# Chunk 0 of a fused attention and MoE kernel in two parts, with chunk 1 between them

## The chip, the cores and the metric

The kernel runs on one core of one Trainium2 chip. The metric is the device time of one execution, in microseconds (us); the profile of one execution gives a span from its first to its last instruction, which is a little shorter than the device time. Engines are named as the profile names them: PE (TensorE, matmuls), DVE (VectorE), ACT (ScalarE), POOL (GpSimd) and SP (SyncE, which here issues the DMAs).

## The reference

Four batches of eight heads, 576 positions, head width 64. Each head's output is a local attention (a band of seven positions) plus a coarse attention over means of four positions, repeated fourfold. The result, 2304 tokens of 512, goes through a two-layer MLP with a Mish-like gate; its weights are float64.

```python
def _attn_ref(q, k, v):
    ...
    q_d = q.reshape(B, H, Sd, factor, D).mean(axis=3)
    ...
    out_up = np.repeat(sm_attn(q_d, k_d, v_d), factor, axis=2)
    mask = np.abs(pos[:, None] - pos[None, :]) < factor
    scores = np.where(mask, scale * np.matmul(q, k.transpose(0, 1, 3, 2)), -1000000000.0)
    ...
    return (out_up + np.matmul(attn, v)).astype(np.float32)

def _moe_ref(x, w_in, w_out):
    h = x @ w_in
    sp = np.where(h > 20.0, h, np.log1p(np.exp(np.minimum(h, 20.0))))
    return ((h * np.tanh(sp)) @ w_out).astype(np.float32)
```

## The kernel before, in words

Attention is done in units of one batch and one pair of heads (four pairs a batch, 16 units). A unit loads `qk` and `vv` by DMA (L417, L503), reduces and scores on PE (`sc`, `sl`), does both softmaxes on DVE and ACT, lets POOL sum `vv` (L506, L508, into `vd`), transposes (`at`, `pt`, `pve`) and multiplies on PE (`pvo`, and L566, 72 small matmuls into `pve` and `pvo`). DVE adds both parts (L579), ACT rounds the sum to the high part of x (L597) and DVE subtracts for the low part (L599). From the fifth unit on all units share one set of buffers, so a unit's `vv` can be loaded only when the unit before has done its L566.

The MLP runs over six chunks of 384 tokens and 16 tiles `f` of 128 hidden columns. Batch 0 (576 tokens) is chunk 0 and the first half of chunk 1; batch 1 is the other half of chunk 1 and chunk 2. Chunks 0 and 1 go in *slots*, one slot a chunk and an `f`: 12 matmuls `h<-x,wi` (four pairs times three combinations of high and low parts, L785), Mish and its high part on ACT (L809, L814), the low part on DVE (L815), and nine matmuls `acc<-wo,g` (L828) into three PSUM banks, which hold a chunk's sums from its first `f` to its last. After the last `f` ACT and DVE copy the banks to `stg` tiles and SP stores them (L838 to L844). Chunks 2 to 5 go in *quartets*, a Strassen scheme of seven products (L746), with the sums of x made from chunks in DRAM (`far`, `sa`, `fars`, `q`).

A weight tile comes as 64-bit words. For each `wi` and `wo` of an `f`: one DMA of 512 KB (L628), ACT scales the high words (L630), DVE shifts the low ones (L632), joins both (L634, into an `stg` tile `full`), ACT or DVE makes the rounded high part (L640 or L638), DVE the low part (L641). Seven `stg` tiles are shared with the outputs and the sums.

The order of the instructions on every engine is written out by a planner inside the kernel: each operation has an assumed duration, a due time (`prio`, in slots) and its dependences, and the planner picks on each engine the due operation that can run. The constants at the head of the file (ATT, UNIT, WPRI, LAG and so on) shift the due times. Where PE would idle in the plan, it puts fillers: matmuls on the identity (`warm`, 512 columns, before the first slot; 128 columns into the unused end of an `h` bank after it). The order is fixed when the program is built; on the chip the engines wait for each other by semaphores. Each engine, and SP's list of DMAs, takes its own in order.

Of the kernel before, what the change touches and what calls it, by code (L numbers as in the profile page):

```python
# [9 lines left out]
F32 = mybir.dt.float32  # L10
# [5 lines left out]
ALU = mybir.AluOpType  # L16
# [3 lines left out]
P = 128  # L20
BIG = 1e30
CH = 384
LAG = (0.1, 6.06, 26.18)
FA = 5
SETS = 3
ATT = {0: (-842.3, 62.6), 1: (2.8, 3.8), 2: (-7.2, 5.7), 3: (-35.9, 5.6)}
WPRI = (-2.33, 7.84, 15.62)
UNIT = {(0, 0): -55, (1, 3): -15, (0, 3): 10, (1, 2): -8, (0, 2): 23, (1, 1): -38, (0, 1): 67, (1, 0): 5, (3, 3): 8, (2, 3): -11, (3, 2): 0, (2, 0): 2, (2, 2): 12, (3, 0): 2, (2, 1): 5, (3, 1): -22}
WARM = True
NPRO = 4  # L30
WACT = 184
STICK = 34
VOFF = 1
WDMA = -65
PIPE0 = (1, 0, 1)
PIPE1 = (1, 0, 1)
LEAD = 3
PMASK = (0, 1)
AMUL = ((0, 2), (1, 0), (1, 1))
AEXP = ((0, 2),)  # L40
WHI = ((0, 'wo'), (2, 'wo'), (7, 'wi'), (8, 'wi'), (11, 'wi'), (12, 'wi'), (14, 'wo'), (15, 'wi'), (15, 'wo'))
RDV = ((0, 0), (0, 1), (0, 2), (0, 3), (1, 0), (1, 3), (2, 0), (3, 0), (3, 2), (3, 3))
GHI = (9, 10, 12, 13, 14, 16, 17, 18, 20, 23, 24, 25, 30)
NMISH = (4,)
TAIL = 0
SPRE = 44
SPRE2 = 104
JPRE = -45
XDMA = -45
QPRE = -15  # L50
QPRE2 = 100
QSTEP = 0.6
QDMA = 51
SUMS = 2
TPRE = 92
UPRE = -20
KEEP = 121
LOAD, PRE = 1320, 250
TICK, BUSY, PACE = 3413.3, 3900, 4900
KW = 38  # L60
RATE, LAND = 415.0, 1100
# [35 lines left out]
class Plan:  # L97
# [9 lines left out]
    def op(self, eng, dur, fn, r=(), w=(), prio=None, after=(), cold=None, cols=0, gap=0, two=True, ins=6, tab=None):  # L107
        o = Op()
        o.eng, o.dur, o.fn, o.cold, o.cols, o.gap, o.two, o.ins, o.tab = eng, dur, fn, cold or 2 * dur, cols, gap, two, ins, tab
        o.prio = self.prio if prio is None else prio  # L110
        o.deps, o.bufs, o.outs, o.seq, o.raw, o.hold = set(after), [], [], len(self.ops), set(), 0.0
        for items, writes in ((r, False), (w, True)):
            for x in items:
                b, key = x if isinstance(x, tuple) else (x, None)
                write = writes or b.group.endswith("ps")
                if b not in o.bufs:
                    o.bufs.append(b)
                    b.left += 1
                for k, (wr, rd) in b.marks.items():
                    if key is None or k is None or k == key:  # L120
                        o.deps.update(wr)
                        o.raw.update(wr)
                        if write:
                            o.deps.update(rd)
                if write:
                    if key is None:
                        b.marks = {None: ({o}, set())}
                    else:
                        b.marks[key] = ({o}, set())
                else:  # L130
                    b.marks.setdefault(key, (set(), set()))[1].add(o)
        o.deps.discard(o)
        self.ops.append(o)
        return o
# [192 lines left out]
def dve(n, fast=False):  # L327
    return 69 + (0.52 if fast else 1.042) * n
# [10 lines left out]
class Kernel:  # L339
# [59 lines left out]
    def attention(self, b, p, sb, ps, padded, loose):  # L399
# [62 lines left out]

        pmask = b in PMASK or (b, p) in AEXP

# [149 lines left out]
    def load_w(self, f):  # L614
# [6 lines left out]
        for nm, src in (("wi", wi), ("wo", wo)):  # L621
            pl.prio = prio + (WPRI[2] if nm == "wo" else 0)
            raw = pl.buf("wa" if f < FA else "wb", f"{nm}{f}", [P, 512, 2], I32, 1, f"raw_{nm}{f}")
# [6 lines left out]
            op("act", act(512), lambda hi=hi: nc.scalar.activation(  # L630
                hi().bitcast(F32), hi().bitcast(F32), AF.Prelu, scale=2.0 ** -112, alpha=2.0 ** 32), w=[h], prio=pl.prio + WACT, tab="exp")
            op("dve", dve(512, True), lambda lo=lo: nc.vector.tensor_scalar(  # L632
# [158 lines left out]
    def tail(self, s, c, f, h, own=None, place=("mish", "g"), last=None):  # L791
        nc, pl = self.nc, self.plan
        op = pl.op
        last = f == self.NF - 1 if last is None else last
        if own is None:
            G, psum = pl.buf("mish", "mA", [P, CH], F32, NMISH[0], f"mA{s}"), True
            Gv, Hv = G, h
            H, h = [[(b, m) for m in range(3)] for b in (G, h)]
        else:
            H, Gv, Hv, psum = h, own, own, False  # L800
        g = pl.buf(*place, [P, 2, CH], F32R, 3 if place[0] == "x" else 2, f"g{s}")
        parts = [(0, CH, None)] if s < 95 - TAIL else [(i * P, (i + 1) * P, i) for i in range(3)]

        for c0, c1, key in parts:
            n, o_ = c1 - c0, slice(c0, c1)
            pl.prio = s + 0.2
            x_, h_ = [b if key is None else [b[key]] for b in (H, h)]
            one, two = [(g, 2 * (key or 0) + j) for j in range(2)]
            op("act", act(n, psum), lambda o_=o_: nc.scalar.activation(Gv()[:, o_], Hv()[:, o_], AF.Mish),  # L809
               r=h_, w=x_, tab="mish")  # L810
            if s in GHI:
                op("dve", dve(n, True), lambda o_=o_: nc.vector.tensor_copy(g()[:, 0, o_], Gv()[:, o_]), r=x_, w=[one])
            else:
                op("act", act(n), lambda o_=o_: nc.scalar.activation(g()[:, 0, o_], Gv()[:, o_], AF.Copy), r=x_, w=[one])  # L814
            op("dve", dve(n), lambda o_=o_: nc.vector.tensor_tensor(  # L815
                out=g()[:, 1, o_], in0=Gv()[:, o_], in1=g()[:, 0, o_].bitcast(F32), op=ALU.subtract), r=[*x_, one], w=[two])
        wo = self.w["wo", f]
        first = c not in self.acc
        if first:
            where, tag = ("attps", "att1") if c in (3, 5) else ("moeps", None)  # L820
            self.acc[c] = [pl.buf(where, tag or f"acc{i}", [P, 512], F32, self.nb[where, tag] if tag else 1, f"acc{s}_{i}")
                           for i in range(3)]
        for i in range(3):
            a_ = self.acc[c][i]

            def mm2(i=i, a_=a_, first=first, last=last):
                for j, (a, b_) in enumerate(((0, 0), (0, 1), (1, 0))):
                    nc.tensor.matmul(a_(), g()[:, a, i * P:(i + 1) * P], wo()[:, b_],  # L828
                                     start=first and j == 0, stop=last and j == 2)

            gi = [g] if len(parts) == 1 else [(g, 2 * i), (g, 2 * i + 1)]
            op("pe", 700, mm2, r=[*gi, wo], w=[a_], cols=1536, prio=s + LAG[(s >= 20) + (s >= 60)] - 0.5 + 0.1 * i)
            if not last:
                continue
            o = pl.buf("stg", "stg", [P, 512], F32, self.nstg, f"o{c}_{i}")
            ov, ok = o, o
            if i % 2:
                op("dve", dve(512), lambda a_=a_, ov=ov: nc.vector.tensor_copy(ov(), a_()),  # L838
                   r=[a_], w=[ok], prio=s + 1, two=False)
            else:  # L840
                op("act", act(512, True), lambda a_=a_, ov=ov: nc.scalar.activation(ov(), a_(), AF.Copy),
                   r=[a_], w=[ok], prio=s + 1)
            r0 = c * CH + i * P
            op("sp", P * 2048 / RATE, lambda r0=r0, ov=ov: nc.sync.dma_start(self.out[r0:r0 + P, :], ov()), r=[ok], prio=s + 1)  # L844

    def run(self, ctx):
        tc = self.tc
        nc, pools = self.nc, {}
# [27 lines left out]
        for b in (0, 1):  # L876
            for p in range(self.NPAIR):
                if len(units) == NPRO:
                    break
                units.append((ATT[b][0] + ATT[b][1] * p + UNIT.get((b, p), 0), self.attention(  # L880
                    b, p, sets[len(units) % len(sets)], ("props", "attps"),
# [2 lines left out]
        gate = list(pl.ops)  # L884
        n0 = len(pl.ops)
        for f in range(self.NF):
            pl.prio = WPRI[0] + WPRI[1] * f
            self.load_w(f)

        todo = [(c, f) for c in range(2) for f in range(self.NF)]  # L890
        s = 0

        def slots(todo):
            nonlocal s
            for c, f in todo:
                self.slot(s, c, f)
                s += 1

        def units(bs):
            us = [(ATT[b][0] + ATT[b][1] * p + UNIT.get((b, p), 0), self.attention(b, p, "att", "attps", probs["att"], False))  # L900
                  for b in bs for p in range(self.NPAIR) if 4 * b + p >= NPRO]
            self.record(us, PIPE1)

        units((1,))
        slots(todo[:16])
        units((2, 3))
        self.sums(2)
        slots(todo[16:32])
        self.operands(2)
        for i in range(self.NF // 2):  # L910
            self.quartet(32 + 4 * i, i, 2)
# [84 lines left out]
```

## Time and profile before

| what | us |
|---|---|
| median of three runs | 497.84 (495.67 to 500.41) |
| the profiled execution's own time | 497.26 |
| its span, first to last instruction | 495.5 |

The profile lists for each engine the time in which it was busy and what ended its idle time. Matmuls overlap, so a row of n matmuls starts the next row a little before its own end; PEld are weight loads, which run beside the matmuls. "PEclk" is the granted clock as a share of 2.4 GHz. Names are `out<-in`, with the buffer numbers left out.

### The profile page before, as it was taken

To read this page: it belongs to the slowest core of one execution; us is meant where nothing else is said; L and a number is where in the kernel's file an instruction comes from. 1 tells how busy PE (TensorE), PEld (TensorE's weight loads), DVE (VectorE), ACT (ScalarE), POOL (GpSimd) and SP (SyncE) were. 2 spreads that over 40 slices of the span, in tenths; PEclk is the share of its full clock that TensorE was granted. 3 is DMA by queue.
4 is the path that set the end of the run, shared out by engine and by line. 5 is a ranking of instruction groups with operands and counts; after the bars stand their busy time and mean duration, and the time that the engine had idled before them with its cause. 6 is when DMAs were issued, how large, how long until landed. Compare 5 with 4: busy or idle time off the path is not lost.

```text
span 495.5 us, 11601 instructions
## 1 busy us (share of the span) xinstructions
PE 479.5 (97%) x4728; PEld 412.8 (83%) x4728; DVE 361.2 (73%) x821; ACT 281.2 (57%) x642; POOL 43.5 (9%) x70
## 2 busy tenths in 40 slices
PE   7889999999999999999999999999999999999996
PEld 3667877878788888888898999889989999888885
DVE  4999998999975586667896867656949877653511
ACT  2598999858575597766544334334735444343411
POOL 7501001112021111011000000000000000000000
PEclk9999999999999999999999999999999999999999
DMA  8976996355444687525311410101430000000003
GB/s 344 419 291 243 411 413 244 123 176 179 141 142 155 216 276 243 194 69 182 105 32 33 141 36 16 33 16 39 123 127 1 0 2 1 1 0 1 0 1 127
DMA packets 23381, 65.60 MB, mean 132 GB/s; under 512 B 2592, under 2 KB 12832, under 8 KB 21280
## 3 DMA queue, kind: packets, MB, share of 16 engines
q1 hardware_dynamic: 23328, 64.86, 36.3%
q8 instruction: 37, 0.61, 0.5%
q14 instruction: 16, 0.13, 0.1%
HBM read 53.84 MB, written 11.01 MB: 131 GB/s over the span
## 4 chain that ended last, share of the span: by engine, by line
PE 81%; ACT 9%; DVE 7%; issue 2%; POOL 1%; ACTq 0%; DVEq 0%; POOLq 0%
PE acc L828 37%; PE h L746 24%; PE h L785 9%; PE sc L433 2%; PE pve L566 2%; PE sl L472 2%; PE pt L551 1%; ACT raw_wi L630 1%; ACT L809 1%; PE pvo L538 1%; ACT raw_wo L630 1%; PE at L517 1%; DVE qkd L418 1%; ACT mA L809 1%; ACT A L440 1%
## 5 line engine op out<-in xcount | busy, mean ns | idle before, releaser
L828 PE MATMUL acc<-wo,g 128*128 128x512 f32 x864 | 219.3, 395 | 0.0
L828 PEld LDWEIGHTS acc<-wo,g 128*128 128x128 f32 x864 | 159.3, 188 | 28.4 <-issue 0.4
L753 DVE TENSOR_TENSOR u<-h,u 128x384 f32<-128x384 f32 x112 | 61.0, 552 | 30.6 <-ACT g L814 14.8
L785 PE MATMUL h<-x,wi 128*128 128x384 f32 x384 | 75.6, 344 | 2.4 <-ACT mA L809 1.4
L785 PEld LDWEIGHTS h<-x,wi 128*128 128x128 f32 x384 | 66.0, 188 | 5.6 <-ACT mA L809 2.1
L814 ACT ACTIVATE g<-u 128x384 fp32r<-128x384 f32 (+1 forms) x66 | 33.6, 513 | 57.5 <-PE acc L828 57.1
L809 ACT ACTIVATE u<-u 128x384 f32<-128x384 f32 (+1 forms) x66 | 33.8, 515 | 52.0 <-DVE u L753 51.8
L815 DVE TENSOR_TENSOR g<-u,g 128x384 fp32r<-128x384 f32 (+1 forms) x66 | 35.4, 541 | 35.0 <-ACT g L814 35.0
L746 PE MATMUL h<-x,t 128*128 128x384 f32 x192 | 39.9, 338 | 0.6 <-DVE u L753 0.6
L506 POOL TENSOR_TENSOR vv<-vv 128x512 f32<-128x512 f32 x16 | 22.8, 1423 | 184.0 <-DMA vv<-in_vv_dram 144.1
L746 PE MATMUL h<-x,wi 128*128 128x384 f32 x192 | 38.7, 337 | 0.0
L718 ACT ACTIVATE t<-b 128x256 fp32r<-128x256 f32 x64 | 26.4, 414 | 21.3 <-PE h L746 16.6
L746 PEld LDWEIGHTS h<-x,t 128*128 128x128 f32 x192 | 34.1, 188 | 3.1 <-DVE u L753 1.2
L746 PEld LDWEIGHTS h<-x,wi 128*128 128x128 f32 x192 | 34.1, 188 | 1.0
L746 PE MATMUL h<-sfar,t 128*128 128x384 f32 x144 | 32.0, 342 | 0.0
L418 DVE TENSOR_REDUCE qkd<-qk 128x288 f32<-128x1152 f32 x16 | 21.5, 1343 | 11.2 <-DMA qk<-in_qk_dram 11.1
L719 DVE TENSOR_TENSOR t<-b,t 128x256 fp32r<-128x256 f32 x64 | 26.4, 416 | 3.5 <-ACT t L718 3.2
L746 PEld LDWEIGHTS h<-sfar,t 128*128 128x128 f32 x144 | 25.6, 188 | 2.8 <-DVE u L753 0.8
L715 DVE TENSOR_TENSOR b<-b,b 128x256 f32<-128x256 f32 x64 | 26.9, 421 | 1.2
L709 DVE TENSOR_TENSOR b<-wi 128x256 f32<-128x256 f32 x64 | 25.7, 418 | 0.8
L815 DVE TENSOR_TENSOR g<-mA,g 128x384 fp32r<-128x384 f32 x32 | 18.3, 581 | 9.9 <-ACT g L814 9.7
L440 ACT ACTIVATE A<-sc,cst 128x144 f32<-128x144 f32 x48 | 18.0, 379 | 12.0 <-DVE cst L438 11.9
(115 smaller groups left out, 690.7 us busy)
## 6 DMA issues: line engine op xcount, KB each, us to landing
vv<-in_vv_dram SPq DMA_DIRECT2D x16, 1152.0 KB, 5.9
qk<-in_qk_dram SPq DMA_DIRECT2D x16, 582.0 KB, 6.5
raw_wi<-in_w_in_dram SPq DMA_DIRECT2D x16, 512.0 KB, 10.4
raw_wo<-in_w_out_dram SPq DMA_DIRECT2D x16, 512.0 KB, 10.3
out_dram<-o SPq DMA_DIRECT2D x18, 256.0 KB, 2.1
sa<-far SPq DMA_DIRECT2D x16, 192.0 KB, 2.6
fars<-sa SPq DMA_DIRECT2D x16, 192.0 KB, 2.9
q<-fars SPq DMA_DIRECT2D x16, 192.0 KB, 3.0
```

What stands on the lines that cost most here:

```text
L418: op("dve", dve(2 * S), lambda: nc.vector.tensor_reduce(out=qkd().rearrange("p (a t) -> p a t", a=2), in_=qk()[:, :, 3:3 + S].rearrange("p ...
L709: op("dve", dve(n), lambda k=k, w=w, c=c: nc.vector.tensor_tensor(out=t[k](), in0=w()[:, 0, c:c + n].bitcast(F32), in1=w()[:, 1, c:c + n]. ...
L715: op("dve", dve(n), lambda ko=ko, a=a, b_=b_: nc.vector.tensor_tensor(out=t[ko](), in0=t[a](), in1=t[b_](), op=ALU.subtract), r=[t[a], t[b ...
L718: op("act", act(n), lambda w=w, ko=ko: nc.scalar.activation(w()[:, 0], t[ko](), AF.Copy), r=[t[ko]], w=[(w, 0)])
L719: op("dve", dve(n), lambda w=w, ko=ko: nc.vector.tensor_tensor(out=w()[:, 1], in0=t[ko](), in1=w()[:, 0].bitcast(F32), op=ALU.subtract), r ...
L746: nc.tensor.matmul(bank()[:, :CH], wv(a, j), xv()[:, b_], start=j == 0 and m == 0, stop=j == 1 and m == 2)
L753: op("dve", dve(CH), lambda: nc.vector.tensor_tensor(out=at[to](), in0=bank()[:, :CH], in1=at[a](), op=ALU.add), r=[bank] + u[a] * (a != t ...
L785: nc.tensor.matmul(h()[:, :CH], w()[:, a, kt * P:(kt + 1) * P], x()[:, b_, :], start=kt == 0 and j == 0, stop=kt == 3 and j == 2)
L809: op("act", act(n, psum), lambda o_=o_: nc.scalar.activation(Gv()[:, o_], Hv()[:, o_], AF.Mish), r=h_, w=x_, tab="mish")
L814: op("act", act(n), lambda o_=o_: nc.scalar.activation(g()[:, 0, o_], Gv()[:, o_], AF.Copy), r=x_, w=[one])
L815: op("dve", dve(n), lambda o_=o_: nc.vector.tensor_tensor(out=g()[:, 1, o_], in0=Gv()[:, o_], in1=g()[:, 0, o_].bitcast(F32), op=ALU.subtr ...
L828: nc.tensor.matmul(a_(), g()[:, a, i * P:(i + 1) * P], wo()[:, b_], start=first and j == 0, stop=last and j == 2)
```

## The change

Chunk 0 is done in two parts. Its first eight `f` tiles come first; then the three banks are copied to `stg` and stored to DRAM (`part`), chunk 1 runs through all 16 tiles, and then chunk 0's last eight tiles run into fresh sums; `part` is loaded back into three `stg` tiles, and DVE adds it to the banks before the output is stored. So the first weights are read by chunk 0 and by chunk 1 before weights 8 to 15 are needed, and x of chunk 1, to which all four units of batch 1 belong, is needed after eight slots instead of 16. The due time of weights 8 to 15 moves by eight slots. All constants of the planner are new, and its order with them. Lines move by 2 or 3 (L579 is L581, L599 is L601, L641 is L643, L785 is L787, L828 is L831).

```diff
-LAG = (0.1, 6.06, 26.18)
+LAG = (0.16, 3.61, 21.98)
...
+CUT = 8
+PART = -7
...
+        cut = c == 0 and f == CUT - 1 and not last
...
-                                     start=first and j == 0, stop=last and j == 2)
+                                     start=first and j == 0, stop=(last or cut) and j == 2)
...
-            if not last:
+            if not last and not cut:
                 continue
-            o = pl.buf("stg", "stg", [P, 512], F32, self.nstg, f"o{c}_{i}")
+            parted = c == 0 and CUT < self.NF
+            pl.loose = parted
+            o = pl.buf("stg", "stg", [P, 512], F32, self.nstg, f"o{c}_{f}_{i}")
+            pl.loose = False
             ov, ok = o, o
-            if i % 2:
+            if parted and last:
+                part = self.away["part", i]
+                op("sp", P * 2048 / RATE, lambda o=o, part=part: nc.sync.dma_start(o(), part()), r=[part], w=[o], prio=s - PART)
+                op("dve", dve(512), lambda a_=a_, o=o: nc.vector.tensor_tensor(out=o(), in0=a_(), in1=o(), op=ALU.add),
+                   r=[a_], w=[o], prio=s + 1, two=False)
+            elif i % 2:
...
+            if cut:
+                self.away["part", i] = part = pl.buf("dram", f"part{i}", [P, 512], F32, 1, f"part{i}")
+                op("sp", P * 2048 / RATE, lambda o=o, part=part: nc.sync.dma_start(part(), o()), r=[o], w=[part], prio=s + 1)
+                continue
...
+        if cut:
+            del self.acc[c]
...
-            pl.prio = WPRI[0] + WPRI[1] * f
+            pl.prio = WPRI[0] + WPRI[1] * (f if f < CUT else CUT + f)
...
-        todo = [(c, f) for c in range(2) for f in range(self.NF)]
+        todo = [(0, f) for f in range(CUT)] + [(1, f) for f in range(self.NF)] + [(0, f) for f in range(CUT, self.NF)]
...
-        slots(todo[:16])
+        slots(todo[:CUT])
         units((2, 3))
+        slots(todo[CUT:CUT + self.NF])
         self.sums(2)
-        slots(todo[16:32])
+        slots(todo[CUT + self.NF:])
```

Three places of the new order matter below. In the names, `h16` is slot 16, `x3_1` is x of pair 3 and chunk 1, `wi0` the first layer's weights of tile 0, `at2_1` a tile of the unit of batch 2 and pair 1, and the last number counts buffers.

PE where chunk 1's first slot begins, before:

```order
L517 MATMUL at2_1_2277<-ident_59,A2_1_2233 128x128 x3
L518 MATMUL at2_1_2277<-ident_59,Ar_att_200 96x128
L785 MATMUL h15_2243<-x2_0_749,wi15_2179 128x384 x3
L785 MATMUL h15_2243<-x3_0_859,wi15_2179 128x384 x3
L785 MATMUL h16_2296<-x0_1_531,wi0_683 128x384 x3
L785 MATMUL h16_2296<-x1_1_632,wi0_683 128x384 x3
L785 MATMUL h16_2296<-x2_1_754,wi0_683 128x384 x3
L785 MATMUL h16_2296<-x3_1_862,wi0_683 128x384 x3
L538 MATMUL pvo2_1_2318<-AT2_1_2287,vd2_1_2309 64x144 x2
```

The same place now, slot 8; the last of batch 1's units, (1,3), is still being worked on:

```order
L787 MATMUL h8_1703<-x0_1_533,wi0_693 128x384 x3
L787 MATMUL h8_1703<-x1_1_634,wi0_693 128x384 x3
L519 MATMUL at1_3_1722<-ident_59,A1_3_1632 128x128 x3
L520 MATMUL at1_3_1722<-ident_59,Ar_att_200 96x128
L787 MATMUL h8_1703<-x2_1_771,wi0_693 128x384 x3
L787 MATMUL h9_1732<-x0_1_533,wi1_818 128x384 x3
L831 MATMUL acc0_0_1003<-wo7_1461,g7_1720 128x512 x3
L831 MATMUL acc0_1_1014<-wo7_1461,g7_1720 128x512 x3
L831 MATMUL acc0_2_1022<-wo7_1461,g7_1720 128x512 x3
L787 MATMUL h9_1732<-x1_1_634,wi1_818 128x384 x3
L787 MATMUL h9_1732<-x2_1_771,wi1_818 128x384 x3
```

Some forty rows on (the unit's last matmuls, the scores of the next unit, and twelve fillers of 128 columns into `h8`) comes the last pair:

```order
L945 LDWEIGHTS ident_59
L945 MATMUL h8_1703<-ident_59 128x128
L787 MATMUL h8_1703<-x3_1_887,wi0_693 128x384 x3
L787 MATMUL h9_1732<-x3_1_887,wi1_818 128x384 x3
L787 MATMUL h10_1943<-x0_1_533,wi2_896 128x384 x3
```

What was one uninterrupted slot, with x made long before, is now two slots that are begun and left open until the last unit's x is there.

DVE where unit (1,3) ends, before:

```order
L698 TENSOR_TENSOR x2_2_1937<-q20_2_1850,x2_2_1937 128x384
L438 TENSOR_SCALAR cst2_0_1939<-cst2_0_1939 128x3
L579 TENSOR_TENSOR x32_1_3_1948<-pve1_3_1874,xd1_3_1871 128x5x64
L579 TENSOR_TENSOR x32_1_3_1948<-pvo1_3_1859,xd1_3_1871 128x4x64
L641 TENSOR_TENSOR wi13_1941<-full_wi13_1896,wi13_1941 128x512
L641 TENSOR_TENSOR wo12_1898<-full_wo12_1887,wo12_1898 128x512
L599 TENSOR_TENSOR x3_1_862<-x32_1_3_1948,x3_1_862 128x192
```

And now:

```order
L643 TENSOR_TENSOR wi10_1811<-full_wi10_1799,wi10_1811 128x512
L440 TENSOR_SCALAR cst2_0_1852<-cst2_0_1852 128x3
L581 TENSOR_TENSOR x32_1_3_1863<-pve1_3_1792,xd1_3_1784 128x5x64
L581 TENSOR_TENSOR x32_1_3_1863<-pvo1_3_1774,xd1_3_1784 128x4x64
L700 TENSOR_TENSOR x2_2_1854<-q20_2_1772,x2_2_1854 128x384
L640 CAST wo10_1915<-full_wo10_1809 128x512
L601 TENSOR_TENSOR x3_1_887<-x32_1_3_1863,x3_1_887 128x192
```

At the end of this unit DVE is at weights 10 instead of 12 and 13: between the first slot's x and this place stand 131 operations of DVE instead of 151.

SP after the cut, now; the stores and two of the three reloads of the partial sums stand ahead of the next unit's `vv`:

```order
L505 DMA vv1_3_1628<-in_vv_dram 128x2304
L419 DMA qk2_0_1696<-in_qk_dram 128x1164
L594 DMA far2_2_1717<-x32_1_2_1630 128x384
L856 DMA part0_1763<-o0_7_0_1751 128x512
L697 DMA q20_2_1772<-far2_2_1717 128x384
L856 DMA part2_1779<-o0_7_2_1767 128x512
L856 DMA part1_1797<-o0_7_1_1782 128x512
L845 DMA o0_15_0_1813<-part0_1763 128x512
L845 DMA o0_15_2_1858<-part2_1779 128x512
L505 DMA vv2_0_1872<-in_vv_dram 128x2304
```

Between the `qk` loads of batch 1's second and third unit SP has 12 weight loads where it had 19.

## Rows read from the trace of the kernel before

**Rows 1.** The page, busy time of two engines (share of the span) and instructions.
```profile
PE 479.5 (97%) x4728; PEld 412.8 (83%) x4728; DVE 361.2 (73%) x821; ACT 281.2 (57%) x642; POOL 43.5 (9%) x70
```

**Rows 2.** Stretches: us, busy us of PE, PEld, DVE, ACT, POOL, clock, DMA share, GB/s.
```profile
42.65:116.30 73.65, 70.36 (x879) 59.82 (x880) 70.94 (x154) 64.63 (x141) 9.20 (x8) 1.00 0.70 266
116.30:241.00 124.70, 123.96 (x1803) 106.91 (x1803) 90.74 (x205) 84.72 (x187) 18.70 (x16) 1.00 0.54 181
241.00:491.70 250.70, 250.11 (x1240) 223.09 (x1238) 166.12 (x384) 105.71 (x230) 0.00 (x0) 1.00 0.11 36
```

**Rows 3.** Waits of PE from 42.65 to 241 us: total us, times, longest.
```profile
PE h L785 <- ACT mA L809: 1.4, 2, 1.2
PE h L785 <- DVE wi L641: 1.0, 1, 1.0
PE at L517 <- DVE A L451: 0.7, 1, 0.7
PE pve L566 <- ACT PT L558: 0.5, 1, 0.5
PE pvo L538 <- POOL vd L508: 0.4, 1, 0.4
```

**Rows 4.** Timeline of PE around the first slot: start us, length us.
```profile
40.99 0.84 PE L472 MATMUL sl<-qk 64*32 64x38 f32 x72
41.77 0.82 PE L927 MATMUL warm<-ident 128*128 128x512 bf16 x3
42.65 4.43 PE L785 MATMUL h<-x,wi 128*128 128x384 f32 x24
...
49.45 4.25 PE L828 MATMUL acc<-wo,g 128*128 128x512 f32 x18
```

**Rows 5.** One stretch, PE alone: us, busy us, clock, DMA share, GB/s.
```profile
42.65:113.20 70.55, 67.26 (x793) 1.00 0.72 276
```

**Rows 6.** Timeline of DVE from the first slot's x on: start us, length us.
```profile
42.29 0.81 DVE L599 TENSOR_TENSOR x<-x,x 128x384 fp32r<-128x384 f32 x2
...
43.52 0.68 DVE L634 SCALAR_TENSOR_TENSOR full_wi<-raw_wi 128x512 int32<-128x512 int32 x1
44.12 0.50 DVE L490 TENSOR_TENSOR L_att<-sl,lst 128x342 f32<-128x342 f32 x1
44.54 0.68 DVE L641 TENSOR_TENSOR wo<-full_wo,wo 128x512 fp32r<-128x512 f32 x1
...
45.21 0.42 DVE L632 TENSOR_SCALAR raw_wi<-raw_wi 128x512 int32<-128x512 int32 x1
45.55 0.17 DVE L445 RECIPROCAL cst<-cst 128x3 f32<-128x3 f32 x1
```

**Rows 7.** Timeline of DVE at the end of unit (1,3).
```profile
115.16 0.47 DVE L579 TENSOR_TENSOR x<-pve,xd 128x320 f32<-128x320 f32 x1
...
117.09 0.34 DVE L599 TENSOR_TENSOR x<-x,x 128x192 fp32r<-128x192 f32 x1
```

**Rows 8.** Timeline of DVE, three operations that waited or ran long.
```profile
77.56 1.35 DVE L418 TENSOR_REDUCE qkd<-qk 128x288 f32<-128x1152 f32 x1 [1.85 <-DMA qk<-in_qk_dram]
...
89.40 1.66 DVE L641 TENSOR_TENSOR wo<-full_wo,wo 128x512 fp32r<-128x512 f32 x1
90.98 1.09 DVE L451 TENSOR_TENSOR A<-A,cst 128x384 f32<-128x384 f32 x1
```

**Rows 9.** Timeline of POOL, the sums of one unit.
```profile
89.21 1.30 POOL L506 TENSOR_TENSOR vv<-vv 128x512 f32<-128x512 f32 x1 [10.82 <-DMA vv<-in_vv_dram]
90.59 1.07 POOL L508 TENSOR_TENSOR vd<-vv 128x256 f32<-128x256 f32 x1
```

**Rows 10.** Stretches of the prologue, PE alone: us, busy us, clock, DMA.
```profile
19.30:20.70 1.40, 0.17 (x19) 1.00 1.02 408
20.70:22.60 1.90, 1.72 (x87) 1.00 1.04 425
22.60:26.05 3.45, 3.45 (x23) 0.51 1.03 410
26.05:42.65 16.60, 14.64 (x360) 1.00 0.56 213
```

More of the change, by code (lines that the diff above doesn't have):

```diff
@@ L22 @@
 CH = 384
-LAG = (0.1, 6.06, 26.18)
+LAG = (0.16, 3.61, 21.98)
 FA = 5
 SETS = 3
-ATT = {0: (-842.3, 62.6), 1: (2.8, 3.8), 2: (-7.2, 5.7), 3: (-35.9, 5.6)}
-WPRI = (-2.33, 7.84, 15.62)
-UNIT = {(0, 0): -55, (1, 3): -15, (0, 3): 10, (1, 2): -8, (0, 2): 23, (1, 1): -38, (0, 1): 67, (1, 0): 5, (3, 3): 8, (2, 3): -11, (3, 2): 0, (2, 0): 2, (2, 2): 12, (3, 0): 2, (2, 1): 5, (3, 1): -22}
+ATT = {0: (-867.6, 83.3), 1: (8.8, 3.4), 2: (-7.9, 1.5), 3: (-38.7, 4.8)}
+WPRI = (6.24, 15.95, 13.25)
+UNIT = {(0, 0): -56, (1, 3): -23, (0, 3): 30, (1, 2): -12, (0, 2): 18, (1, 1): -25, (0, 1): 79, (1, 0): -6, (3, 3): 10, (2, 3): -7, (3, 2): 14, (2, 0): -5, (2, 2): 3, (3, 0): -18, (2, 1): -1, (3, 1): -13}
 WARM = True
 NPRO = 4
[L31 to L34, printed above, removed]
+WACT = 67
+STICK = 53
+VOFF = 3
+WDMA = -72
 PIPE0 = (1, 0, 1)
@@ L38 @@
 PMASK = (0, 1)
[L39 to L43, printed above, removed]
+AMUL = ((0, 2), (0, 3), (1, 0))
+AEXP = ((0, 2), (1, 0))
+WHI = ((0, 'wo'), (1, 'wi'), (2, 'wi'), (4, 'wo'), (6, 'wi'), (6, 'wo'), (7, 'wi'), (8, 'wi'), (8, 'wo'), (9, 'wi'), (10, 'wo'), (11, 'wo'), (13, 'wi'), (14, 'wi'))
+RDV = ((0, 1), (0, 2), (1, 2), (1, 3), (2, 1), (2, 2), (3, 1))
+GHI = (1, 3, 4, 7, 10, 11, 15, 16, 19, 23, 28, 30)
 NMISH = (4,)
 TAIL = 0
[L46 to L51, printed above, removed]
+CUT = 8
+PART = -7
+SPRE = 6
+SPRE2 = 114
+JPRE = -52
+XDMA = -82
+QPRE = 31
+QPRE2 = 68
 QSTEP = 0.6
-QDMA = 51
+QDMA = 85
 SUMS = 2
-TPRE = 92
-UPRE = -20
-KEEP = 121
+TPRE = 114
+UPRE = -34
+KEEP = 154
 LOAD, PRE = 1320, 250
```

## The prediction

> **What bounds the kernel now.** I read the busy shares first [rows 1]: TensorE (PE) is busy 97% of the span, VectorE (DVE) 73%. That is an average, so the stages come next [rows 2]. From 241 us to the last matmul at 491.7 us PE is busy 250.11 of 250.70 us and DVE 166; the change leaves that stage's work as it is, and only a PE with less to do could shorten it. From 116.3 to 241 us PE is busy 123.96 of 124.70 us, again no room. From 42.65 us, where the first slot's matmuls start, to 116.3 us PE lacks 3.29 us, and DVE (70.94 of 73.65) is as full as PE. So the kernel is bound by PE everywhere, and in this one stage DVE is level with it. The waits of PE over both slot stages [rows 3] say what is to be had at most: 1.4 + 1.0 + 0.7 + 0.5 + 0.4 = 4.0 us, 0.8% of the span; all but the 0.7 lie before 113.2 us. PE's work itself is the same before and after: the same matmuls, cut into one more accumulation.
>
> **The change, part by part.** Sum made against the profiled execution's own time, 497.26 us (span 495.5 and 1.8 around it); the median of the runs is 497.84, 0.6 above it, so the forecast is good to about that.
>
> *The start.* Between the last loads of attention and the first `h` the new order has eight `warm` matmuls where the old one has three, and one fewer further up. A `warm` costs 0.82 / 3 = 0.27 us at most [rows 4], so four more are 0.9 to 1.1 us, if nothing else moves; DVE's order has `sl1`'s reduce and two weight operations more ahead of the subtraction that ends x of the last pair, and less of others, about 1.3 us by their starts (0.60 for a 128x512 operation of two inputs, 0.34 for a shift [rows 6]). Part of this lies in time in which PE idled anyway. I take 0.6 us later, so the first `h` at 43.2 and this subtraction at 42.9 instead of 42.29; bounds -0.3 and +1.3.
>
> *Batch 1 is now due at slot 8.* Slot 8 needs x of all four pairs of batch 1. In the old order `x3_1` (made by L579, L597, L599 from the last pair) is written 60 matmul groups before `h16` reads it. In the new one only filler, the scores of the next unit and three quarters of two `h` stand between the pair's last matmuls and `h8<-x3_1`. So here PE waits for DVE, and the question is who gets there when.
>
> DVE: from the subtraction of the first slot to the first L579 of pair (1,3) the old kernel takes 115.16 - 42.29 = 72.87 us for 151 operations [rows 6, 7]. The new order has 131 in the same stretch. Counted by kind it lacks six L634 and five L641 (0.60 each, start to next start: 44.12 - 43.52, and L641 is as long, 0.68), seven L632 (0.34: 45.55 - 45.21), four L815 (some 0.47, a 384 wide L641) and has three more casts L638 (0.33, like the shift) and two L812; the other kinds, one up or one down, net 0.9 less: 6.6 + 2.4 + 1.9 - 1.0 - 0.5 + 0.9 = 10.3 us. So 62.6 us if DVE loses as much to others as before. It loses to two things that the trace shows: a wait for `qk` of 1.85 us [rows 8] (0.25 another time), and POOL: while POOL adds `vv` at 89.21 and 90.59 us [rows 9], L641 takes 1.66 us instead of 0.68 and L451 1.09 [rows 8], about 1.5 us a unit, seen twice in full and once in part. The `qk` load of the third pair now has 12 weight loads ahead of it instead of 19, so I strike the 2.1 us of waits; POOL's four sums remain. That makes 60.5 us: L579 at 42.9 + 60.5 = 103.4 us. From there to the end of the last subtraction it is 117.09 + 0.34 - 115.16 = 2.3 us [rows 7]; `x3_1` is there at 105.7. Bounds: 55.5 us with every loss gone (100.7), 64.1 with all of them and one more collision with POOL (109.3).
>
> One page of the Trainium skill bears on the loss: SBUF — State Buffer, section SBUF: two separate sides, calls the port pair of VectorE and GpSimd "an **exclusive lock**, not a bandwidth split"; by it four units lose at most four times the two POOL operations, 2.4 us each, 9.6 us, where my rows make it about 4. The trace agrees that one blocks the other; with the rule's most `x3_1` would come 5 us later still.
>
> PE: from 42.65 to 113.20 us, just before the last matmuls of pair (1,3), it is busy 67.26 of 70.55 us [rows 5]. Up to `h8<-x3_1` the new order has 39 `h` matmuls less (114 for 153, 4.43 / 24 = 0.185 each [rows 4]: 7.2 us), 21 `acc` matmuls less (72 for 93, 4.25 / 18 = 0.23: 4.8), and one block of 72 small matmuls of `pve`/`pvo` and one of `sl` more, 0.84 each by the `sl` row, 1.7. So 57.0 us of work, and PE is at the door at 43.2 + 57.0 = 100.2 us. It waits 105.7 - 100.2 = 5.5 us in all, mostly at this place (bounds 0.5 and 9.1), against the 3.3 us that the old order lost before 113.2. The twelve small fillers (128 columns) lie in that idle time and cost nothing.
>
> *What hangs on the wait.* Behind `h8<-x3_1` on PE stand the second `h`, the next unit's transposes and the first `acc` of chunk 1; nobody but PE's own followers waits for them, and DVE and ACT go on with weights.
>
> *The partial sums.* Three evacuations (two on ACT, one on DVE, L838's kind), six DMAs of 256 KB and three DVE additions in place of three evacuations. The additions are not in the old trace; the nearest row is L641 (0.68), a bank read may make it 0.5 to 0.8: 2 us of DVE at the end of chunk 0, in a stage where DVE is busy 90.74 of 124.70 us [rows 2] and each acc bank is next needed some fifteen matmuls after its last. Cost taken 0; at worst PE waits for one addition and what is queued before it, 1.5 us. On SP the two reloads stand ahead of `vv` of the next unit and wait for the stores to land; at forecast times `vv` is issued some 3 us before PE gets past the door, and its sum is read 8 us of matmuls behind the door: 0, at worst 2 us. Three of seven `stg` tiles are held for chunk 0's end; weights use them one after the other on DVE, so 0.
>
> *Weights 8 to 15* are due eight slots later. That frees DVE, but not PE, which had only 0.7 us of waits behind 116 us; I keep these.
>
> Sum: +0.6 (start) + 5.5 (door) - 3.3 (waits of the old order in the same work) = +2.8 us: 497.26 + 2.8 = **500.1 us**.
>
> **The rivals.**
> *A, slower: the door costs the clock too.* At 19.3 us PE did 0.17 us of work in 1.40 us, and from 22.6 us the granted clock was 0.51, half of 2.4 GHz, for 3.45 us; before and after it is 1.00 [rows 10]. If the wait at the door is like that, and DVE is at the late bound, then 9.1 us of waiting in place of 5.5 (+3.6) and half of a 3.45 us stretch (+1.7): 505.4 us. It decides where DVE loses more than about 7 us to POOL and loads. For it: two of DVE's losses are as large as the rival needs, and the filler is thin, twelve matmuls of 128 columns. Against: a single wait of 1.4 us led to it in a stretch with little else on PE; at the door `sc` and `sl` stand in between.
> What the skill says on this, in TensorE: Matmul & The Clock Gate, section Why this matters for your kernels, is that idle gaps between bursts of matmuls bring back the half rate; no run shown here has such a gap within the slots, so the rival's price stands on rows 10 alone.
> *B, quicker: DVE gains all it can.* `x3_1` at 100.7, the wait at the door 0.5 us, the old waits gone: 0.6 + 0.5 - 3.3 = -2.2, 495.1 us; with the later 0.7 gone as well and an earlier start (-0.3 instead of 0.6), 493.5. For it: DVE's 20 operations less. Against: POOL's sums, which all remain and now lie closer together. More than 4.0 us of waits are not there to be removed, so over 1% faster is nearly excluded.
> *C, the detour over DRAM holds up the next unit:* SP's two waits delay `vv`, and with it the next unit's `vd`, by up to 2 us, and one addition delays a bank 1.5 us: 503.6 us. Against: both have slack of several us above.
>
> **How the numbers follow.** Forecast 0.57, A 0.18, B 0.17, C 0.08. Over 1% (5 us, about what a measurement of this kernel can tell from no change): faster needs 492.9, beyond even B's 493.5, 0.05 with the spread of runs; slower needs 502.8, which A and most of C reach, and the forecast's upper tail: 0.24. The rest, 0.71, is no change. The range goes from B's late end, 494, to A's 505.5.
>
> **What would show it.** Right: PE's waits list led by `h` L787 waiting for DVE's x (L601) once, 3 to 7 us, near 100 us; first `h` near 43; PE without further gaps to the end; DVE full to 105 us. Wrong: no such wait, or several of 1 us and more after slot 8, or a wait at the change of acc banks near chunk 0's end; a granted clock under 1 near 105 us speaks for A, `pvo` waiting for POOL's `vd` of the next unit for C.

## The result, and the profile after

| | us |
|---|---|
| changed kernel, median of four runs | 502.42 (501.88 to 505.52) |
| kernel before, median of its runs beside it | 496.99 (495.67 to 500.41) |
| ratio | 1.0115, interval 1.0081 to 1.0149 |
| the profiled execution: its own time, span | 505.52, 503.5 |

The change makes the kernel 1.1% slower. The forecast was 500.1 us, with 494.0 to 505.5 as the range: the time lies inside it, on the side that was forecast, and 2.3 us above the value. Run again later, the changed kernel took 502.08 us (six runs) beside 497.58 for the kernel before, ratio 1.0098 (1.0065 to 1.0131).

The profiled execution is the longest of the four, and one thing in it has to be taken out first. Stretches of the changed kernel, PE alone; the columns are start and end, length, busy us (matmuls), granted clock, DMA share and GB/s:

```profile
0.00:22.00 22.00, 17.13 (x394) 1.00 0.93 376
22.00:34.80 12.80, 12.77 (x174) 0.51 0.93 370
34.80:47.37 12.57, 11.32 (x267) 0.96 0.24 65
```

In this execution PE ran at half its clock (1.2 of 2.4 GHz) from 22 to about 35.7 us; in that of the kernel before it was 3.45 us [rows 10]. The first `h` comes at 47.37 us instead of 42.65. This length changes from execution to execution of either kernel: the mean clock over a span was 0.985 to 1.00 before and 0.986 to 1.00 after. Executions with a mean clock of 1.00 took 495.71 us before and 501.16 and 501.31 after, 5.5 us more; at a mean clock of 0.997 fourteen executions before took 496.89 us in the mean and four after 502.06. So the change costs 5.2 to 5.5 us at equal clock. A profile of experiment 3 below, whose start has the same instructions but for four fillers, has 3.4 us of half clock and its first `h` at 43.65 us; that of the changed kernel in experiment 8, with all its fillers, has 3.4 us and 43.58. At equal clock the start is 0.9 to 1.0 us later.

From the first `h` to the last matmul the changed kernel takes 499.88 - 47.37 = 452.51 us, the kernel before 491.71 - 42.65 = 449.06: 3.45 us more. The same view from the first `h` on:

```profile
47.37:106.60 59.23, 55.10 (x721) 1.00 0.85 328
106.60:113.90 7.30, 5.85 (x180) 1.00 0.79 273
113.90:246.00 132.10, 131.66 (x1776) 1.00 0.48 161
246.00:382.00 136.00, 135.45 (x677) 1.00 0.21 66
382.00:499.88 117.88, 117.81 (x579) 1.00 0.02 7
```

PE's idle time is 59.23 - 55.10 = 4.13 us up to the last unit's end, 1.45 us at the door of slot 8, 0.44 in the rest of the slots and 0.62 in the quartets, 6.6 in all; before it was 3.29 [rows 5], 0.74 behind 113.2 us (what is left of the 4.03 of [rows 2]) and 0.59, 4.6 in all. To these 2.0 us come 1.0 us of the twelve fillers at the door; 0.45 us of busy time are left, and where they lie was not traced. So the waits in the old order's place have not gone, and the door has come on top. The waits of PE from 47 to 385 us, against [rows 3]:

```profile
PE h L787 <- ACT mA L812: 3.6, 4, 1.1
PE sc L435 <- ACT PT L556: 0.6, 1, 0.6
PE at L520 <- DVE Ar_att L456: 0.6, 1, 0.6
PE h L748 <- DVE u L755: 0.6, 1, 0.6
PE acc L831 <- issue: 0.4, 1, 0.4
PE sl L474 <- DVE x L581: 0.3, 1, 0.3
PE at L519 <- DVE A L453: 0.2, 1, 0.2
```

No row names DVE's `x` of L601, which was to lead this list with 3 to 7 us. ACT's `mA` leads it: PE waits for Mish before it may write a bank again. The third of these four waits, on ACT and on PE:

```profile
71.24 0.68 ACT L632 ACTIVATE raw_wo<-raw_wo 128x512 f32<-128x512 f32 x1
71.80 0.23 ACT L532 ACTIVATE R_att<-at 16x96 f32<-16x96 f32 x1
72.04 1.28 ACT L812 ACT_TABLE_LOAD   x1
73.34 0.49 ACT L812 ACTIVATE mA<-h 128x384 f32<-128x384 f32 x1
```

```profile
69.89 2.85 PE L787 MATMUL h<-x,wi 128*128 128x384 f32 x15
73.88 1.31 PE L787 MATMUL h<-x,wi 128*128 128x384 f32 x6 [1.14 <-ACT mA L812]
```

ACT works off weights, then loads the table for Mish in 1.28 us, then computes `mA`; PE's next `h` starts when it is done. And the door itself, on PE (the rows of L568 left out) and on DVE:

```profile
105.79 0.47 PE L540 MATMUL pvo<-AT,vd 128*64 128x144 f32 x4
...
106.50 0.63 PE L553 MATMUL pt<-ident,L_att 128*128 128x128 f32 x4
106.96 0.27 PE L559 MATMUL pve<-ident,L_att 128*38 128x128 f32 x1
107.88 0.82 PE L435 MATMUL sc<-qkd 64*64 64x144 f32 x9 [0.64 <-ACT PT L556]
...
109.89 0.62 PE L945 MATMUL h<-ident 128*128 128x128 bf16 x8
110.80 0.84 PE L474 MATMUL sl<-qk 64*32 64x38 f32 x72 [0.29 <-DVE x L581]
111.58 0.40 PE L945 MATMUL h<-ident 128*128 128x128 bf16 x4
111.78 1.56 PE L787 MATMUL h<-x,wi 128*128 128x384 f32 x6
113.87 0.79 PE L787 MATMUL h<-x,wi 128*128 128x384 f32 x3 [0.53 <-ACT mA L812]
```

```profile
110.27 0.48 DVE L581 TENSOR_TENSOR x<-pve,xd 128x320 f32<-128x320 f32 x1
110.67 0.41 DVE L581 TENSOR_TENSOR x<-pvo,xd 128x256 f32<-128x256 f32 x1
...
111.80 0.35 DVE L601 TENSOR_TENSOR x<-x,x 128x192 fp32r<-128x192 f32 x1
```

Read them by their starts. PE issues the last unit's transposes `pt` at 106.50, right behind DVE's L500 (105.85 to 106.35), whose result they read, and comes to `h<-x3_1` at 111.78; DVE's L581 starts 0.3 us after the last L568 matmul has ended (109.96). DVE isn't idle there either; DVE alone in a stretch up to L581:

```profile
99.80:110.27 10.47, 10.47 (x25) 1.00 0.62 219
```

L581 starts when DVE's own order comes to it, behind weights and small operations. So the door is not one long wait of PE for DVE's x: PE has to do the unit's last pieces itself, each waits for the one before by way of ACT or DVE, and both engines come to L581 within 0.3 us of each other. Which of the two sets the time there this trace alone doesn't tell. Between `pt` and the third `h` PE has the scores of the next unit and fillers to put there, and nothing else, since both `h` banks hold slots that lack the last pair.

### The profile page after: what moved, and what is told of

It reads as the page before. It is cut to its first block, busy times and chain, and to the rows that moved or that the text cites. A ratio compares the mean times of both kernels' runs of the same rounds, so it can differ in the third digit from the quotient of the medians.

```text
span 503.5 us, 11635 instructions
## 1 busy us (share of the span) xinstructions
PE 487.1 (97%) x4744; PEld 417.9 (83%) x4744; DVE 362.7 (72%) x825; ACT 279.3 (55%) x663; POOL 50.5 (10%) x70
## 4 chain that ended last, share of the span: by engine, by line
PE 83%; ACT 8%; DVE 6%; issue 1%; POOL 1%; ACTq 0%; DVEq 0%; POOLq 0%
PE acc L831 37%; PE h L748 24%; PE h L787 10%; PE pve L568 2%; PE sc L435 2%; PE sl L474 2%; PE pt L553 1%; ACT raw_wi L632 1%; ACT raw_wo L632 1%; PE at L519 1%; PE pvo L540 1%; PE warm L945 1%; ACT L812 1%; PE pvo L568 1%; DVE full_wo L636 1%
## 5 line engine op out<-in xcount | busy, mean ns | idle before, releaser
L831 PE MATMUL acc<-wo,g 128*128 128x512 f32 x864 | 220.8, 395 | 0.5 <-issue 0.4
L831 PEld LDWEIGHTS acc<-wo,g 128*128 128x128 f32 x864 | 159.1, 188 | 28.9 <-issue 1.0
L755 DVE TENSOR_TENSOR u<-h,u 128x384 f32<-128x384 f32 x112 | 61.2, 553 | 35.7 <-PE h L748 32.8
L787 PE MATMUL h<-x,wi 128*128 128x384 f32 x384 | 76.0, 343 | 3.7 <-ACT mA L812 3.6
L787 PEld LDWEIGHTS h<-x,wi 128*128 128x128 f32 x384 | 66.3, 188 | 7.3 <-ACT mA L812 4.8
L508 POOL TENSOR_TENSOR vv<-vv 128x512 f32<-128x512 f32 x16 | 29.0, 1814 | 169.1 <-DMA vv<-in_vv_dram 130.2
L748 PE MATMUL h<-x,wi 128*128 128x384 f32 x192 | 41.4, 337 | 0.0
L568 PEld LDWEIGHTS pve<-PT,vv 38*64 38x64 f32 x640 | 22.4, 142 | 3.3 <-ACT PT L560 1.8
L568 PE MATMUL pve<-PT,vv 38*64 38x32 f32 x640 | 24.5, 227 | 0.3 <-ACT PT L560 0.2
```

The lines of the kernel that those rows point to most:

```text
L508: op("pool", gps(512), lambda: nc.gpsimd.tensor_tensor(out=vc()[:, :, 0:2], in0=vc()[:, :, 0:2], in1=vc()[:, :, 2:4], op=ALU.add), w=[(vv, ...
L568: nc.tensor.matmul(o_()[64 * h:64 * h + 64, c0:c0 + 32], vw()[64 * e:64 * e + KW, j, f, 64 * h:64 * h + 64], PT()[64 * e:64 * e + KW, j, 6 ...
L748: nc.tensor.matmul(bank()[:, :CH], wv(a, j), xv()[:, b_], start=j == 0 and m == 0, stop=j == 1 and m == 2)
L755: op("dve", dve(CH), lambda: nc.vector.tensor_tensor(out=at[to](), in0=bank()[:, :CH], in1=at[a](), op=ALU.add), r=[bank] + u[a] * (a != t ...
L787: nc.tensor.matmul(h()[:, :CH], w()[:, a, kt * P:(kt + 1) * P], x()[:, b_, :], start=kt == 0 and j == 0, stop=kt == 3 and j == 2)
```

## The experiments

Four theories run through the experiments. *S*: the loss is the later start, the door and waits that stayed. *L*: the door costs the latency of the unit's end, because PE has nothing else there. *T*: the waits in the first slots are ACT's table loads. *D*: DVE's pace to the last pair's x sets everything, so what is saved elsewhere comes back as a wait for DVE. Others (K, P, Q, F, G, W, and the prediction's A and C) belong to one experiment each; the text ahead of the run says what they are.

**1. The changed kernel again** (no edit).

> The changed kernel once more, for a second profile. Theory S (the 5 us are made of a later start and of waits and fillers in the slots): the first h comes at 44 to 45 us when the half clock at the start lasts the 3.5 us it lasted in the kernel before, the stretch from the first h to the last matmul takes 452.5 us again (within 0.7; the kernel before: 449.1), and the time is 501.5 to 503. Rival K (the new order itself brings the long half clock): the granted clock is 0.5 for over 10 us again, the first h comes at 47 or later, and the time is over 504.

502.08 us (501.16 to 505.55); from the first `h` to the last matmul 499.91 - 47.49 = 452.42 us. The stretch repeats within 0.1 us. The profiled execution again had the long half clock, as K has it, but the other five did not (mean clocks 0.986 for the profiled one, then 0.993, 0.997, 0.997, 1.00, 1.00). The times fit S; that the half clock is no property of the order rests on the clocks of these runs and on experiments 2 to 4, whose first `h` came at 42.4 to 43.7 us.

**2. No fillers at the door.**

```diff
-            fn, n = (lambda first=b.todo == 4: self.filler(b()[:, CH:], first)), 512 - CH
+            fn, n = (lambda: None), 512 - CH
```

> The changed kernel without the twelve 128-column fillers at the door of slot 8, order otherwise the same. Theory S: the fillers lie in time in which PE would wait anyway: same time within 0.5 us, and PE's idle time from 106.9 to 113.6 us of the profile grows by about 1 us from 1.2. Rival F (the fillers are work on the path): 1.1 us faster at the door. Rival A of the prediction (idle PE loses its clock): granted clock under 1 within 5 us behind the door, 1 to 2 us slower.

501.58 us, ratio to the kernel before 1.0087 (1.0053 to 1.0121): the same time. Stretches of this kernel around the door, PE alone:

```profile
101.60:109.30 7.70, 5.80 (x168) 0.89 0.81 276
...
108.00:109.00 1.00, 1.00 (x5) 0.50 0.98 406
109.00:110.40 1.40, 1.40 (x6) 0.50 1.06 307
110.40:112.00 1.60, 1.60 (x10) 0.78 0.86 314
```

PE idles 1.90 us here instead of 1.45, and its clock falls to half for 3.4 us; with the fillers the granted clock stayed at 1.00 across the door, in the two profiles of the changed kernel and in those of experiments 3, 4 and 8. From the first `h` to the last matmul this kernel takes 495.76 - 42.37 = 453.39 us, 0.9 us more than with the fillers. So the fillers aren't on the path (F falls): they cost 1.0 us of busy time and save about twice that in waits and clock. Rival A of the prediction was right on the mechanism, though its 1 to 2 us don't show in the time, and the twelve thin fillers are what kept it out. The Trainium skill, in TensorE: Matmul & The Clock Gate, section Why this matters for your kernels, warns of long idle gaps between bursts of matmuls, which bring the half rate back. This trace agrees that idle time does it, but has no long gap: the largest single wait before the fall was 0.84 us.

**3. Four fillers less ahead of the first slot.**

```diff
+            count = [0]
...
+                count[0] += t is None
+                if t is None and count[0] > 32:
+                    return
                 t = warm if t is None else t
```

> The changed kernel with four of the eight 512-column fillers ahead of the first h left out. Theory G (the first h waits for DVE's last operations on the prologue's PSUM, not for the fillers): the first h moves by less than 0.3 us (42.4 us where the clock is full up to there), same time within 0.5 us. Rival W (the fillers are what makes the start late): the first h 0.9 us earlier, the time 0.9 us less.

501.16 us (500.15 to 503.83), ratio 1.0080 (1.0049 to 1.0111). That is 0.9 us less than in experiment 1, as W has it, but the intervals overlap; the trace has to decide. PE's wait at the first `h`, at 43.65 us:

```profile
PE h L787 <- DVE lst L482: 1.0, 1, 1.0
```

PE now waits 1.0 us for what the fillers had covered: the wait ends with DVE's L482, a small operation of the next batch's first unit that stands just behind L581 of batch 0's last pair (43.08 to 43.50). With all eight fillers and the same half clock the first `h` came at 43.58 (experiment 8). So theory G holds, and the four fillers of the prediction's sum only fill. The start is later because DVE has more to do ahead of this place: before the subtraction that ends the first slot's x it is busy 34.52 us with 85 operations, where it was 32.99 us with 80.

**4. No detour over DRAM.** Stores and reloads of `part` are left out, and the additions are copies, so chunk 0's output lacks its first eight `f` tiles.

```diff
-                op("sp", P * 2048 / RATE, lambda o=o, part=part: nc.sync.dma_start(o(), part()), r=[part], w=[o], prio=s - PART)
-                op("dve", dve(512), lambda a_=a_, o=o: nc.vector.tensor_tensor(out=o(), in0=a_(), in1=o(), op=ALU.add),
+                op("sp", P * 2048 / RATE, lambda: None, r=[part], w=[o], prio=s - PART)
+                op("dve", dve(512), lambda a_=a_, o=o: nc.vector.tensor_copy(o(), a_()),
...
-                op("sp", P * 2048 / RATE, lambda o=o, part=part: nc.sync.dma_start(part(), o()), r=[o], w=[part], prio=s + 1)
+                op("sp", P * 2048 / RATE, lambda: None, r=[o], w=[part], prio=s + 1)
```

> The changed kernel without the stores and reloads of the partial sums, and with plain copies in place of the three additions (it leaves out the first eight f tiles' part of chunk 0's output). Theory S: same time within 0.6 us of the changed kernel (502.1), PE's waits unchanged: the detour lies beside other work. Rival C of the prediction (the detour delays the next unit's vv, or the additions a bank): 1.5 to 3.5 us faster.

503.13 us (500.61 to 504.3); from the first `h` to the last matmul 495.01 - 42.38 = 452.63 us, 0.1 us more than the changed kernel, and the waits are led by the same row (3.6 us for `mA`). The time is 1.0 us above experiment 1's, not within the 0.6 of S, but nothing is won. Stores, reloads and additions are free; rival C falls. The copies of the three banks at the cut remain in this kernel, so what they cost it doesn't tell.

**5. The new constants without the split, and the split with the old constants.** First the changed kernel with the cut at the end, then the changed kernel with every other constant of the kernel before (the first of them shown).

```diff
-CUT = 8
+CUT = 16
```

```diff
-LAG = (0.16, 3.61, 21.98)
+LAG = (0.1, 6.06, 26.18)
...
```

> All new constants, but chunk 0 in one piece (the cut at 16). Theory S: the door at slot 8 with its fillers and waits (2.3 us in the profile) is gone, the later start stays: 499 to 500.5, with no filler in an h bank. Rival P (the split costs nothing, the new constants plan a worse order): 502 or more. Rival Q (the split alone costs): 497 as before, with the first h at 42.7.

> The split with all constants of the kernel before. Theory S: the old due times bring x of the last pair of batch 1 for slot 16, now it is needed at slot 8, so PE waits at the door longer than with the new constants: over 5 us there, 502 to 510. Rival P: 497 to 499, since the old constants plan the better order.

525.73 us, ratio 1.0563 (1.0536 to 1.0591), and 514.55 us, 1.0344 (1.0299 to 1.0389). S's numbers were wrong by 25 us for the first and by 4.6 for the second; P's (502 or more) is met by the first, but its 497 to 499 is far from the second. So this doesn't separate the order from the split: the first kernel fails somewhere else. The largest wait of the first kernel:

```profile
PE h L748 <- ACT sfar L699: 15.7, 1, 15.7
```

Its quartets start before the sums of x are loaded. In the second kernel the planner put 120 fillers (9.0 us busy) where the changed kernel has 12, and PE still waits 2.1 us for L581 at the door. Neither half of the change does for itself, and of the cuts tried here (8, 9, 10, 12 and 16) the constants fit the one at eight only.

**6. The cut two and four tiles later** (10 in the first kernel, 12 in the second).

```diff
-CUT = 8
+CUT = 10
```

> The changed kernel with the cut after ten f tiles instead of eight, all other constants as they are. Up to the last unit of batch 1 the order is the same on PE and DVE; behind it two slots of chunk 0 (8 and 9) stand where the changed kernel begins slots 8 and 9 of chunk 1, and no filler is left in an h bank. Theory L (the door costs the latency of the unit's end, from its last transposes to x, because PE has nothing else to do): the 2.3 us of idle time and fillers at 107 to 114 us go, the time is 499.3 to 500.5, the waits for ACT's mA before the door stay at 3 us or more. Rival D (DVE's pace sets x of the last pair and everything behind): PE waits as much a little later, for weights 8 and 9 or for x, and the time stays at 501.5 to 502.5.

> The cut after twelve f tiles. Theory L: nothing more to win over the cut after ten, 499.3 to 500.5. Rival D: each two slots later give DVE more time: 1 to 2 us faster than the cut after ten.

511.31 us, 1.0278 (1.0245 to 1.0311), and 523.45 us, 1.0518 (1.0489 to 1.0547). All forecasts missed, by 8.8 us and more. At ten the door is gone, as L has it; behind a wait at 84.55 us PE's next one is of 0.3 us at 119.96. Yet from the first `h` to the first matmul of the quartets PE idles 5.83 us, where it was 6.02 in the changed kernel. And waits of 1.8, 1.3 and 1.6 us stand at 247 to 256 us, at the start of the quartets, and the granted clock is 0.50 from 250 to 257. At twelve it is 8.5 us for `sfar` in one piece.

**7. The cut one tile later.**

```diff
-CUT = 8
+CUT = 9
```

> The cut after nine f tiles, all other constants as in the changed kernel. Slot 8 is then chunk 0's and its matmuls stand between the last unit's last pieces, no filler is left. Theory L: the 2.3 us of the door go; what the wait for sfar at the start of the quartets gives back is between nothing (the cut after eight) and the 4.9 us of the cut after ten, so 499.5 to 503. Rival D: the waits come up later in the slots and the time is 502 or more even without a wait in the quartets.

509.80 us, 1.0258 (1.0225 to 1.0291), outside L's 499.5 to 503. Stretches of this kernel at the door and at the start of the quartets, PE alone:

```profile
106.00:114.00 8.00, 7.87 (x148) 1.00 0.85 258
...
245.00:250.00 5.00, 3.02 (x14) 1.00 0.80 240
250.00:253.00 3.00, 0.52 (x2) 0.50 0.34 124
253.00:256.00 3.00, 3.00 (x11) 0.50 0.24 67
```

One slot of chunk 0 between the unit's last pieces covers the door but for 0.13 us: L holds at this place. DVE's L581 comes even later after the first `h` than in the changed kernel, 107.23 - 43.38 = 63.85 us instead of 110.27 - 47.37 = 62.90, and PE doesn't wait for it. But D's other half shows behind the door. The waits of PE from 114 us to the quartets, where the changed kernel has none for DVE:

```profile
PE at L519 <- DVE A L453: 1.1, 1, 1.1
PE at L520 <- DVE Ar_att L456: 0.8, 2, 0.7
PE acc L831 <- DVE g L818: 0.2, 1, 0.2
PE pt L553 <- DVE L_att L500: 0.2, 1, 0.2
```

From the first `h` to the first matmul of the quartets PE idles 6.10 of 194.53 us here, and 6.02 of 194.09 in the changed kernel: the idle time that left the door is back as waits for DVE before the quartets begin, and only the 1.0 us of fillers is saved. Then 4.46 us of idle time follow from 245 to 253 us, and some 4.4 us of work at half clock. Without both an estimate from these rows is 509.8 - 4.5 - 2.2 = 503.1 us, which is D's 502 or more and not a gain over 502.1. The planner makes a new order for each cut, so this is one order's result and no proof for D. SP's queue shows why the sums are late there, first of this kernel, then of the changed one:

```profile
239.38 1.82 SPq L697 DMA_DIRECT2D q<-fars  x4
244.64 1.02 SPq L859 DMA_DIRECT2D out_dram<-o  x2
245.79 0.36 SPq L697 DMA_DIRECT2D q<-fars  x1
246.39 0.33 SPq L859 DMA_DIRECT2D out_dram<-o  x1
246.85 1.32 SPq L697 DMA_DIRECT2D q<-fars  x3
```

```profile
240.38 6.94 SPq L697 DMA_DIRECT2D q<-fars  x7
250.29 3.29 SPq L859 DMA_DIRECT2D out_dram<-o  x3
```

With the cut at nine, four of the loads `q` stand behind chunk 0's output stores in SP's queue, and these wait for DVE's three additions at the very end of chunk 0 (243.92 to 246.36 us). With the cut at eight all eight are issued before the stores. Output tiles and loads take turns in the same seven `stg` tiles, which is probably why the planner mixes them; that was not tried.

**8. No table loads in the first eight slots,** in either kernel. ACT copies in place of Mish there, so the gate is missing for chunk 0's first eight `f` tiles. Six table loads fall away in the changed kernel and eight in the kernel before.

```diff
-            op("act", act(n, psum), lambda o_=o_: nc.scalar.activation(Gv()[:, o_], Hv()[:, o_], AF.Mish),
+            op("act", act(n, psum), lambda o_=o_: nc.scalar.activation(Gv()[:, o_], Hv()[:, o_], AF.Copy if s < 8 else AF.Mish),
```

> The changed kernel with a plain copy on ACT in place of Mish in slots 0 to 7 (it leaves the gate of chunk 0's first eight f tiles out), so that ACT loads no table there: six loads of 1.28 us less before 80 us, order otherwise the same. Theory T (the three waits of PE for mA of 3.1 us in the first slots are ACT's table loads): they fall under 0.5 us, the stretch from the first h to the last matmul falls from 452.5 to 449.5 to 450.5, and the time to 499 to 500. Rival D (DVE sets the pace to the door, so PE waits there instead): the waits for mA go, others of 2 to 3 us come up to 112 us, same time within 0.8 us.

> The same edit in the kernel before (plain copies in place of Mish in slots 0 to 7). Theory T: its waits for mA were 1.4 us in two places, so no more than 1.4 us are won: 495.7 to 497. Rival D, for the kernel before: no change, since PE waits for DVE instead: 497.1.

Changed kernel: 500.22 us (ratio to the kernel before 1.0056, 1.0038 to 1.0073), 1.9 us less than with Mish; from the first `h` to the last matmul 494.29 - 43.58 = 450.71 us, 1.8 less. Kernel before: 496.57 us, 0.9978 (0.9959 to 0.9997); 491.86 - 43.97 = 447.89 us, 1.2 less. PE's waits from 43 to 113 us of the changed kernel with the edit:

```profile
PE sl L474 <- issue: 1.1, 1, 1.1
PE h L787 <- ACT mA L812: 0.7, 2, 0.5
PE pt L553 <- DVE L_att L500: 0.7, 2, 0.5
...
PE pvo L540 <- POOL vd L510: 0.6, 2, 0.4
```

The waits for `mA` fall from 3.6 to 0.7 us, of which 0.5 are the door's. T holds, though its ranges for the stretch and the time are missed by 0.2 us each, and only 1.8 of 3.1 us reach the end: the other 1.3 come back, most of it as an "issue" wait (1.05 us at 76.96 us), the rest for DVE and POOL. To that extent D has a part here too. The table loads of the first slots cost both kernels something; by these profiles the new order pays 0.6 us more, by the times 1.9 against 0.4 us, with intervals too wide to tell more.

## Why the prediction came out as it did

The forecast was +2.8 us on own time; measured are +5.0 by the means of two medians each (502.08 and 502.42 against 497.58 and 496.99) and 5.2 to 5.5 at equal clock. The prediction named a sign that would show it wrong, "no such wait" of PE for DVE's x of L601, and that is what the waits show: the time lies in the range, the mechanism that was to bring it there did not come out. Point by point:

- *The start,* forecast +0.6: measured +1.0 at the same length of half clock. The cause that I had put first, four more fillers, is none (experiment 3); the other, DVE's longer order, is (1.5 us more busy time, forecast 1.3).
- *The waits of the old order,* forecast -3.3: this step failed. Up to the last unit's end PE idles 4.13 us where it was 3.29. I had taken the old waits as belonging to the old order and set no new ones in their place; but an order with the same units and the same banks has such waits of its own, three of them about 1 us long for ACT's `mA`. In the kernel before there were two, 1.4 us in all.
- *The wait up to the door,* forecast 5.5 us "in all, mostly at this place": up to 111.78 us it is 4.1 + 0.9 us of waits and 1.0 us of fillers, 6.0, and another 0.5 behind it. The amount is about right, the place is not: only 1.45 us of idle time and the fillers lie at the door. The picture of a PE that arrives at 100.2 and a DVE that brings x at 105.7 could not happen, because `pt`, L568 and the rest of the unit's end are PE's own instructions ahead of the door: PE can't come earlier than they allow. What was left was the latency from `pt` by way of ACT to L568, and from there by way of L581, ACT's rounding and L601 to `h`, with DVE's own order level with it.
- *PE's work up to the door,* forecast 57.0 us: measured 59.36 less 1.0 of fillers, 58.35. The block of 72 small matmuls, priced at 0.84 by the `sl` row, takes 1.35 us in the kernel before (34.37 to 35.72); the rest of the difference was not traced. So `h<-x3_1` starts 64.41 us after the first `h`, where the forecast had 105.7 - 43.2 = 62.5.
- *DVE's time,* forecast 60.5 us from the first slot's last subtraction to L581: measured 110.27 - 47.88 = 62.39, for the 131 operations. The two waits for `qk` are gone, as assumed; 3.7 us of waits for ACT stand in their place (`g` 1.8, `mA` 0.9, `x` 0.7 and 0.3).
- *Costs at nothing:* the detour and the additions cost nothing, as taken (experiment 4). No wait names the late weights 8 to 15. DVE's copy of one bank at the cut (0.68 us at 106.27) stands in its order 4 us ahead of L581; no run leaves it out.
- *The rivals:* A's loss of clock didn't happen in the kernel as it is, and does in experiment 2. B asked for DVE to gain all; it didn't. C fell.

By the row from the first `h` to the last matmul the sum is: start 1.0, waits before the door +0.84, door 1.45 + 1.0, waits behind it -0.3, the rest of the busy time 0.45, together 4.4 us. Another 0.25 us lies outside the span (505.52 - 503.5 = 2.0 instead of 1.76), and 0.2 us less behind the last matmul: 4.5 of the 5.0 measured. That the forecast came within 2.3 us is luck in part: a gain that didn't come was balanced by a door that was half as long. To more than 1% slower the forecast gave 0.24; the measured 1.0115 (1.0081 to 1.0149) leaves open on which side of that line the change lies.

Open: what the 0.45 us of busy time are; how much of the door is PE's own latency and how much DVE's pace, since closing it brought the idle time back further on; and whether constants made for a cut at nine would do without the waits behind it. In the runs made here no version of the change beats the kernel before.

## What to carry to other kernels

A wait that moves from one place of an order to another is priced by the chain that ends there, and on that chain the waiting engine's own instructions count too: ask what else it can do between them, not only when the other engine is done. When an order is planned anew, don't count the old order's small waits as won: here the new order had its own, for the same banks and the same table loads. And follow a wait that has been closed further down the order: one slot more at the door moved its idle time to waits for DVE later on, and cost more at the quartets than it gained.

## What was not expected of the hardware

- Twelve matmuls of 128 columns, 1.0 us in all, kept the granted clock at 1.00 over a stretch in which PE idled 1.45 of 7.30 us; without them PE idled 1.90 of 7.70 us and the clock fell to 0.50.
- POOL's sum of `vv`, 1.30 us in [rows 9], takes 3.0 to 3.1 us in three units of the changed kernel (at 51.58, 101.10 and 116.18 us); DVE's L643, with two inputs, runs beside it there in its usual 0.68 us. Here it is POOL that is held up, where rows 8 and 9 show DVE held up by POOL. The kernel before has one such case too, 2.62 us at 120.97. That the two engines hold each other up is read from the times, no run tries it.
